# Second batch's rows loaded ahead of the third and fourth expert's weights, and its attention's place in the program worked out anew

## The chip, the cores and the metric

The kernel runs on one core of one Trainium2 chip. The metric is the device time of one execution in microseconds (us). Before the change it is 432.24 us, the median of three runs (428.54, 432.24 and 433.78). The profile shown here is that of one execution whose span, from the first to the last instruction, is 431.1 us.

## The reference

Attention over a sliding window of 128 positions plus four "sink" positions at the start, for 4 batches of 8 heads, 768 positions and 64 elements each. Its output, 3072 rows of 512, goes through four experts, each of two matrix products with a ReLU between; the experts' outputs are weighted and summed.

```python
# attention: q, k, v of shape (4, 8, 768, 64)
scores = (1 / sqrt(64)) * q @ k.transpose(0, 1, 3, 2)
keep   = (pos_k < 4) | ((pos_q - pos_k >= 0) & (pos_q - pos_k < 128))
a      = softmax(where(keep, scores, -1e9))
x      = (a @ v).transpose(0, 2, 1, 3).reshape(3072, 512)

# four experts: w1 (4, 512, 1024), w2 (4, 1024, 512)
p   = domain_probs / domain_probs.sum(-1, keepdims=True)
out = 0
for e in range(4):
    out += p[:, e:e+1] * (maximum(x @ w1[e], 0) @ w2[e])
```

## The kernel before

Everything is computed in bf16 with sums in fp32. The first batch comes in three pieces, is transposed on TensorE, and its attention starts early. The other batches are loaded by rows and transposed by the DMA engines. Batches are numbered from 0, so the second batch is batch 1; experts likewise.

```python
def load_rows(b):                          # batches 1 to 3
    for i, (name, src) in enumerate((("q", q), ("k", k))):
        x = sb.tile([P, NQB, H, D], BF16, name=f"{name}n", tag=f"{name}n", bufs=1)   # one buffer per name
        for tb in range(NQB):              # six loads of 128 KB (as bf16) each
            nc.gpsimd.dma_start(out=x[:, tb], in_=src[b, :, tb*P:(tb+1)*P, :].rearrange("h p d -> p h d"))   # L126
            lands(("rows", b), H * P * D * 4)
        ...
        nc.sync.dma_start_transpose(       # L132: qkT is what scores and sinks read
            out=qkT[b][:, i].rearrange("c t h p -> c (t h) p"),
            in_=x.rearrange("p t h d -> p (t h d)"))
    for hp in range(NHP):
        turned_at[b, 0, hp] = max(landed["rows", b], t["pe"]) + 11000.0

def load_v(b, ts):   ...  nc.gpsimd.dma_start(out=vx[b % 2][:, tb, :, 0:D], ...)     # L195, 128 KB each
def load_w1(e):      ...  nc.gpsimd.dma_start(out=w1_sb[e], ...)                     # L205, 1 MB as bf16
def load_w2(e):      ...  nc.gpsimd.dma_start(out=w2_sb[e], ...)                     # L210, 1 MB as bf16

def regroup(b, piece): ...  # batch 0: reads the same buffers "qn" and "kn" (DVE and ACT copies, L153)
def sink_keys(b):    ...    # POOL, L330: ksd from qkT, the first reader of a batch's transposed keys
def sinks(b, piece): ...    # PE, L349: sink scores from ksd and qkT
def scores(b, hp, g): ...   # PE, L370: window scores from qkT
def values(b, hp, g): ...   # PE, L414 and L421
def turn(b, hp, g):  ...    # PE, L446: gives xT, the experts' input
```

The order of instructions on TensorE is fixed when the program is built. A small model of times (`t`, `landed`, `turned_at`, `bank_free`, in ns) runs along; at each step the loop below emits the piece of work that the model holds to be ready: attention of the next batch ("att"), a first product with its ReLU ("first", L565) or a second product ("second", L600). The chip then runs this order as it stands and waits where the model was too hopeful. The numbers in `turned_at` thus move no data; they say from when on the model lets the batch's attention in.

```python
load_qk(0, 2)
load_v(0, (4, 5))
for e in (1, 2):
    load_w1(e)
    load_w2(e)

mix = Mixture()
att = Attention(0, ...)
while mix.more() or att.more():
    if not att.more() and ahead + 1 < B and (ahead == 0 or mix.done >= cols * ahead):
        ahead += 1
        load_rows(ahead)
        load_v(ahead, range(NQB))
        if ahead == 1:
            load_w1(3)
            load_w2(3)
        att = Attention(ahead, [("sinks", ahead, 0, 0)], range(NG))
        ...
    # ... the piece that the model holds to be ready is emitted
```

Of the kernel before, what the change touches and what calls it, by code (L numbers as in the profile page):

```python
# [16 lines left out]
def kernel(  # L17
# [27 lines left out]
    NQB = S // P  # L45
# [22 lines left out]
    t = {"pe": 0.0, "act": 0.0, "dve": 0.0}  # L68
# [22 lines left out]
    landed = {}  # L91
    dma = {"at": 2500.0}

    def lands(key, nbytes):
        dma["at"] += nbytes / 350.0
        landed[key] = dma["at"] + 1500
# [12 lines left out]
    nat, qkT, turned_at = {}, {}, {}  # L109
# [11 lines left out]
    def load_rows(b):  # L121

        for i, (name, src) in enumerate((("q", q), ("k", k))):
            x = sb.tile([P, NQB, H, D], BF16, name=f"{name}n", tag=f"{name}n", bufs=1)
            for tb in range(NQB):
                nc.gpsimd.dma_start(  # L126
                    out=x[:, tb], in_=src[b, :, tb * P:(tb + 1) * P, :].rearrange("h p d -> p h d"),
                )
                lands(("rows", b), H * P * D * 4)
            if b not in qkT:  # L130
                qkT[b] = sb.tile([P, 2, NQB, NHP, P], BF16, name="qkT", tag="qkT", bufs=2)
            nc.sync.dma_start_transpose(  # L132
                out=qkT[b][:, i].rearrange("c t h p -> c (t h) p"),
                in_=x.rearrange("p t h d -> p (t h d)"),
            )
        for hp in range(NHP):
            turned_at[b, 0, hp] = max(landed["rows", b], t["pe"]) + 11000.0

    def load_first():

# [52 lines left out]
    def load_v(b, ts):  # L193
        for tb in ts:
            nc.gpsimd.dma_start(  # L195
                out=vx[b % 2][:, tb, :, 0:D],
                in_=v[b, :, tb * P:(tb + 1) * P, :].rearrange("h p d -> p h d"),
            )
            lands(("v", b, tb), H * P * D * 4)
# [3 lines left out]
    def load_w1(e):  # L203
        w1_sb[e] = wpool.tile([P, NDB, F], BF16, name=f"w1_{e}", tag=f"w1_{e}")
        nc.gpsimd.dma_start(out=w1_sb[e], in_=moe_w1[e].rearrange("(db p) f -> p db f", p=P))  # L205
        lands(("w1", e), Dm * F * 4)

    def load_w2(e):
        w2_sb[e] = wpool.tile([P, NFB, Dout], BF16, name=f"w2_{e}", tag=f"w2_{e}")
        nc.gpsimd.dma_start(out=w2_sb[e], in_=moe_w2[e].rearrange("(fb p) d -> p fb d", p=P))  # L210
        lands(("w2", e), Dm * F * 4)
# [433 lines left out]
    sink_values(0)  # L645
    load_qk(0, 2)
    load_v(0, (4, 5))
    for e in (1, 2):
        load_w1(e)
        load_w2(e)  # L650

# [6 lines left out]
    ahead, upto, lead = 0, 0.0, 0.0  # L658
    while mix.more() or att.more():
        now = t["pe"]  # L660

        if not att.more() and ahead + 1 < B and (ahead == 0 or mix.done >= cols * ahead):
            ahead += 1
            load_rows(ahead)
            load_v(ahead, range(NQB))
            if ahead == 1:
                load_w1(3)
                load_w2(3)
            att = Attention(
                ahead, [("sinks", ahead, 0, 0)], range(NG),  # L670
            )
            upto = mix.done
        share = (cols * ahead - upto) * 0.96
        due = ahead == 0 or att.steps * share <= (mix.done - upto) * att.total
        opts = []
        if att.more():
            opts = [(max(r, now), 0 if due else 3, "att", step) for r, step in att.options()]
        f, s2 = mix.first_ready(), mix.second_ready()
        opts.append((max(f, now), 2, "first", None))
        opts.append((max(s2, now), 1 if mix.since >= 2 else 2.5, "second", None))  # L680
        r, _, kind, step = min(opts, key=lambda o: (o[0] > now + 40, o[0] if o[0] > now + 40 else 0, o[1]))
        if kind == "att":
            att.emit(step)
        elif kind == "first":
            mix.emit_first()
        else:
            mix.emit_second()
# [35 lines left out]
```

The softmax here doesn't subtract the row's maximum and nothing guards it: scores larger than these inputs give would overflow.

## Time and profile before

| | |
|---|---|
| time, median of three runs | 432.24 us |
| span of the profiled execution | 431.1 us |
| PE busy | 398.3 us (92%) |
| DVE, ACT, POOL busy | 168.1, 169.4, 76.0 us |
| work in the chain that ended last: PE, DMA, POOL | 77%, 17%, 4% |
| longest wait of PE | 15.7 us, once, in L349 |
| first products (L565), second products (L600) | 197.0 us in 1152, 183.0 us in 768 |
| DMA issues of weights, median time to landing | 8 of 1024 KB, 19.4 us |

How to read it: PE is TensorE, PEld its weight loads, DVE VectorE, ACT ScalarE, POOL GpSimd, SP SyncE; SPq is SP's queue, on which the DMA transposes and the output's writes are issued. A PE that is busy for 92% of the span leaves little besides its own work, so what can be won lies in its few idle stretches and in the stretches where its clock is granted at less than full speed. "DMA to landing" is the time from the issue of a transfer until its last part has arrived. Bytes of a transfer are counted as bf16.

### The profile page before, as it was taken

The numbers are of one execution on the slowest core, as the hardware profiler recorded it, in microseconds if no ns is written. First come the engines' busy times: TensorE is split into PE (matmuls) and PEld (weight loads), VectorE is DVE, ScalarE is ACT, GpSimd is POOL, SyncE is SP. The second block draws the span as 40 slices with busy tenths as digits, with TensorE's granted clock in tenths as the row PEclk, the third lists the DMA queues.
The fourth block names the chain that finished last, engine by engine and source line by source line (L and its number), as shares of the span: only waits on it lengthen the run. The fifth ranks groups of instructions, "written<-read, shape, count | busy, mean of one in ns | idle before, by whom it ended". The sixth has DMA issues, their size and how long they took to land.

```text
span 431.1 us, 6810 instructions
## 1 busy us (share of the span) xinstructions
PE 398.3 (92%) x2774; PEld 223.2 (52%) x2774; DVE 168.1 (39%) x348; ACT 169.4 (39%) x331; POOL 76.0 (18%) x124
## 2 busy tenths in 40 slices
PE   7599799049999999999999999999999999999996
PEld 3365466016766654555555554555555555555552
DVE  4667655006655523543434324433434222222222
ACT  3455300007643134454445335534445333333331
POOL 8834470059100007800000001000000000000000
PEclk9599889759999999999999999999999999999999
DMA  9999999999800159910000180000001110000012
GB/s 174 191 195 209 179 139 118 122 120 148 53 0 2 75 156 126 151 9 2 0 2 14 60 205 17 2 1 2 0 2 41 66 44 0 0 2 0 2 49 97
DMA packets 97251, 29.88 MB, mean 69 GB/s; under 512 B 85932, under 2 KB 92076, under 8 KB 97220
## 3 DMA queue, kind: packets, MB, share of 16 engines
q0 software_dynamic: 72832, 17.31, 43.7%
q1 hardware_dynamic: 24388, 12.14, 13.3%
q8 instruction: 21, 0.34, 0.3%
q14 instruction: 10, 0.08, 0.1%
HBM read 35.73 MB, written 6.29 MB: 97 GB/s over the span
## 4 chain that ended last, share of the span: by engine, by line
PE 77%; DMA 17%; POOL 4%; DVE 0%; issue 0%; ACT 0%; ACTq 0%; DVEq 0%; POOLq 0%
PE mop L600 36%; PE hps L565 35%; DMA w<-in_moe_w_dram 9%; DMA qkT<-kn 7%; PE sps L370 3%; PE od L421 2%; POOL vx L195 2%; DMA vx<-in_v_dram 1%; POOL kn L126 1%; PE tx L446 1%; PE od L414 1%; PE sps L349 0%; DVE ht L576 0%; POOL kn L115 0%; POOL qn L115 0%
## 5 line engine op out<-in xcount | busy, mean ns | idle before, releaser
L565 PE MATMUL hps<-xT,w 128*128 128x384 bf16 (+1 forms) x1152 | 197.0, 313 | 0.7 <-DVE ht L576 0.2
L574 ACT ACTIVATE ht<-hps 128x384 bf16<-128x384 f32 (+1 forms) x234 | 109.2, 471 | 188.5 <-PE hps L565 187.2
L600 PE MATMUL mop<-w,ht 128*128 128x512 bf16 x768 | 183.0, 382 | 0.0
L565 PEld LDWEIGHTS <-w 128*128 128x128 bf16 x1152 | 109.4, 99 | 66.5 <-issue 9.4
L600 PEld LDWEIGHTS <-ht 128*128 128x128 bf16 x768 | 73.6, 98 | 79.6 <-issue 4.3
L610 DVE SCALAR_TENSOR_TENSOR out_sb<-mop,scale_t,out_sb 128x512 f32<-128x512 f32 x72 | 54.1, 751 | 140.5 <-PE mop L600 140.1
L381 ACT ACTIVATE aT<-sps 128x1024 bf16<-128x1024 f32 (+1 forms) x46 | 44.0, 957 | 15.9 <-PE sps L370 15.6
L382 DVE TENSOR_TENSOR aT<-aT,mask 128x1024 bf16<-128x1024 bf16 (+1 forms) x46 | 30.0, 652 | 39.8 <-ACT aT L381 39.5
L608 DVE TENSOR_SCALAR out_sb<-mop,scale_t 128x512 f32<-128x512 f32 x24 | 18.0, 750 | 41.4 <-PE mop L600 41.1
L330 POOL TENSOR_TENSOR ksd<-qkT,half 128x8 bf16<-128x8 bf16 x16 | 2.7, 196 | 162.5 <-DMA qkT<-kn 162.5
L576 DVE TENSOR_SCALAR ht<-hps 128x256 bf16<-128x256 f32 (+1 forms) x54 | 23.1, 429 | 11.1 <-PE hps L565 9.3
L421 PE MATMUL od<-vx,aT 128*128 128x65 bf16 x352 | 21.2, 198 | 1.1 <-DVE aT L382 1.1
L195 POOL DMA_DIRECT2D vx<-in_v_dram x24 | 21.5, 960 | 0.0
L431 DVE TENSOR_TENSOR onat<-od,R 128x256 bf16<-128x256 f32 x48 | 20.4, 425 | 1.7
L421 PEld LDWEIGHTS <-aT 128*128 128x128 bf16 x352 | 18.0, 101 | 5.0 <-DVE aT L382 2.0
L446 PE MATMUL tx<-ident,onat 128*128 128x128 bf16 x96 | 13.6, 229 | 6.4 <-DVE onat L431 6.2
L370 PE MATMUL sps<-qkT 64*128 64x128 bf16 (+1 forms) x256 | 18.5, 248 | 1.0 <-ACT aT L381 0.7
L126 POOL DMA_DIRECT2D qn<-in_q_dram x18 | 15.9, 904 | 10.0 <-DVE R L428 8.1
L126 POOL DMA_DIRECT2D kn<-in_k_dram x18 | 15.9, 926 | 8.5 <-ACT aT L381 4.3
L349 PE MATMUL sps<-qkT,ksd 128*32 128x512 bf16 (+1 forms) x20 | 2.5, 390 | 15.7 <-POOL ksd L330 15.7
L153 ACT COPY xT<-tx 128x256 bf16<-128x256 bf16 x25 | 9.1, 373 | 16.6 <-PE tx L446 16.0
L446 PEld LDWEIGHTS <-onat 128*128 128x128 bf16 x96 | 8.3, 99 | 13.3 <-DVE onat L431 7.9
(60 smaller groups left out, 110.8 us busy)
## 6 DMA issues: line engine op xcount, KB each, us to landing
w<-in_moe_w_dram POOLq DMA_DIRECT2D x8, 1024.0 KB, 19.4
out_dram<-out_sb SPq DMA_DIRECT2D x24, 256.0 KB
vx<-in_v_dram POOLq DMA_DIRECT2D x24, 128.0 KB, 5.5
qn<-in_q_dram POOLq DMA_DIRECT2D x18, 128.0 KB, 4.2
kn<-in_k_dram POOLq DMA_DIRECT2D x18, 128.0 KB, 4.6
qraw<-in_q_dram SPq DMA_DIRECT2D x2, 256.0 KB
kraw<-in_k_dram SPq DMA_DIRECT2D x2, 256.0 KB
qn<-in_q_dram POOLq DMA_DIRECT2D x2, 256.0 KB, 9.6
```

Source lines behind the costliest of these rows:

```text
L126: nc.gpsimd.dma_start(out=x[:, tb], in_=src[b, :, tb * P:(tb + 1) * P, :].rearrange("h p d -> p h d"),)
L195: nc.gpsimd.dma_start(out=vx[b % 2][:, tb, :, 0:D], in_=v[b, :, tb * P:(tb + 1) * P, :].rearrange("h p d -> p h d"),)
L370: nc.tensor.matmul(sps[ph][:, c:c + nq * P], lhsT=T[pr, 1, kb, hp, :], rhs=T[pr, 0, qb:qb + nq, hp, :], start=True, stop=True,)
L381: nc.scalar.activation(out=a, in_=both[:, :, 0:w], func=AF.Exp, scale=scale)
L382: nc.vector.tensor_mul(a, a, m[:, None, :].to_broadcast([P, 2, w]))
L421: nc.tensor.matmul(od[:, qi, ph], lhsT=a[:, ph, c:c + P], rhs=vx[b % 2][:, kb, 2 * hp + ph, 0:DX], start=(g == 0 and i == 0), stop=(i == l ...
L446: nc.tensor.transpose(tx[:, qi], o[:, qi], ident)
L565: nc.tensor.matmul(hp_, lhsT=w1_sb[e][:, db, fb * P:(fb + 1) * P], rhs=xT[b, db][:, t0:t0 + n], start=(db == 0), stop=(db == NDB - 1),)
L574: nc.scalar.activation(out=ht, in_=hp_, func=AF.Relu)
L576: nc.vector.tensor_scalar(out=ht, in0=hp_, scalar1=0.0, scalar2=None, op0=ALU.max)
L600: nc.tensor.matmul(op, lhsT=hts[fb][:, off:off + P], rhs=w2_sb[e][:, fb, :], start=(fb == 0), stop=(fb == NFB - 1),)
L610: nc.vector.scalar_tensor_tensor(out=dst, in0=op, scalar=sc, in1=dst, op0=ALU.mult, op1=ALU.add,)
```

## The change

Before, the loads stand on POOL's queue in this order: weights of experts 1 and 2, rows of batch 1, values of batch 1, weights of expert 3. After, the rows and values of batch 1 go ahead of expert 2's weights, so that the transposes and the attention that wait for them can start sooner; the weights of experts 2 and 3 follow. Since the model's landing time of the rows moves forward too, and the weights now follow behind the transposes, the time that the model allows for the transposes of batch 1 is raised from 11,000 to 18,000 ns.

```diff
         for hp in range(NHP):
-            turned_at[b, 0, hp] = max(landed["rows", b], t["pe"]) + 11000.0
+            turned_at[b, 0, hp] = max(landed["rows", b], t["pe"]) + (18000.0 if b == 1 else 11000.0)
@@
     load_qk(0, 2)
     load_v(0, (4, 5))
-    for e in (1, 2):
+    load_w1(1)
+    load_w2(1)
+    load_rows(1)
+    load_v(1, range(NQB))
+    for e in (2, 3):
         load_w1(e)
         load_w2(e)
@@
             ahead += 1
-            load_rows(ahead)
-            load_v(ahead, range(NQB))
-            if ahead == 1:
-                load_w1(3)
-                load_w2(3)
+            if ahead > 1:
+                load_rows(ahead)
+                load_v(ahead, range(NQB))
             att = Attention(
                 ahead, [("sinks", ahead, 0, 0)], range(NG),
             )
```

## The prediction

> **What bounds the kernel now.** I read the page's busy times first: PE is busy for 398.3 of 431.1 us, so only its idle stretches and its slow clock can give anything back. The page's slices show where they are.
>
> ```profile
> PE   7599799049999999999999999999999999999996
> PEclk9599889759999999999999999999999999999999
> ```
>
> Each digit is one fortieth of the span, 10.8 us. From the tenth slice on PE is full. The eighth and ninth digits (0 and 4) are a hole at about 76 to 92 us, and the clock is below full in it and after it. PE's timeline in that stretch gives the hole its cause:
>
> ```profile
> 70.15 3.26 PE L565 MATMUL hps<-xT,w 128*128 128x256 bf16 x24
> 73.25 1.89 PE L600 MATMUL mop<-w,ht 128*128 128x512 bf16 x8
> 74.98 1.04 PE L565 MATMUL hps<-xT,w 128*128 128x256 bf16 x8
> 91.70 1.08 PE L349 MATMUL sps<-qkT,ksd 128*32 128x512 bf16 x4 [15.69 <-POOL ksd L330]
> ```
>
> The bracket says that PE sat idle for 15.69 us until POOL's ksd, which is the first reader of batch 1's transposed keys. The chain of work that ended last, in order of time, tells what POOL waited for:
>
> ```profile
> 24.68 25.02 DMA w<-in_moe_w_dram
> ...
> 58.03 4.54 DMA vx<-in_v_dram
> 62.57 28.74 DMA qkT<-kn
> ```
>
> The first line is w2 of expert 2, issued at 24.68 and landed at 49.70: the rows of batch 1 stand behind it. The last is the DMA transpose of the keys, issued at 62.57 and landed at 91.31. SP's timeline shows both transposes of batch 1 and, for comparison, those of batch 2:
>
> ```profile
> 54.92 7.41 SPq L132 DMA_TRANSPOSE qkT<-qn  x1
> 62.57 15.10 SPq L132 DMA_TRANSPOSE qkT<-kn  x1
> ...
> 155.86 3.04 SPq L132 DMA_TRANSPOSE qkT<-qn  x1
> 159.13 3.06 SPq L132 DMA_TRANSPOSE qkT<-kn  x1
> ```
>
> For batch 2, with no load beside it, POOL's ksd starts at 163.82, so both transposes together took about 163.8 - 155.9 = 7.9 us. For batch 1 they took 91.3 - 54.9 = 36.4 us: the loads of values and of expert 3's weights run beside them. That is the number on which my prediction turns.
>
> The clock costs as well. The table of stages at 2 us a row has the granted clock at 0.50 from 82 to 96 us and at 1.00 from 98. PE works from 91.70, so some 6.1 us of its work ran at half clock, which is a loss of about 3.05 us.
>
> **What the Trainium skill says.** "DMA: Bandwidth & Descriptors", section Queues, rings and completion order: each DMA engine takes turns between the queues that have work, one packet at a time. The trace agrees in kind: the transposes on SP's queue and the loads on POOL's queue both progress between 60 and 82 us, and neither waits for the other to finish (the fifth load of values landed at 73.3, the sixth at 81.8, between the starts and ends of the transposes). "TensorE: Matmul & The Clock Gate", section What's actually happening: the clock is halved after an idle window and comes back after a few us of sustained work, with windows of about 3.4 us. Here it fell some 5 us after the idle began (0.84 in the microsecond from 80) and came back about 6 us after work resumed.
>
> **The change part by part.**
>
> *Work.* No instruction is added or dropped. On PE the two programs have the same matmuls; the order differs only from a place shortly before batch 1's L349 until well into expert 3 of batch 0, after which it is the same.
>
> *When the rows land.* On POOL the rows wait for the buffer qn, which the DVE copy of batch 0's last piece frees (it starts at 32.95 and takes 0.42). Nothing moves that copy, so the first row load is issued near 33.67 as before. What changes is what stands ahead of it in the queue. From the issue times and the times to landing, w1 and w2 of expert 1 landed at 33.9 and 39.65 (22.35 + 17.3), w1 and w2 of expert 2 at 44.6 and 49.70. The last of the six q loads (issued at 39.95, 14.8 us to landing) landed at 54.75, which is 5.05 us behind expert 2's w2. After the change the q rows stand behind expert 1's w2 instead, so they should land 49.70 - 39.65 = **10.05 us earlier**, the last at about 44.7. POOL issues one row load in about 0.9 us and the queue takes them at about 0.87 us each, so issue isn't the limit.
>
> *How long the transposes take.* This is my choice. The same loads as before surround them: first the k rows, then six loads of values, then a w1 and a w2 of 1 MB each (now expert 2's in place of expert 3's), all issued with the same lead over the transposes. In the run before the second of these weights landed at 60.5 + 33.7 = 94.2, after the transposes' end at 91.31, so the load queue was never empty while they ran; the two further megabytes that now follow can't be felt before that point. I therefore keep the whole 36.4 us, not the 18 that the model assumes: end of the key transpose at 91.3 - 10.05 = 81.3, and L349 at 91.70 - 10.05 = **81.65**.
>
> *Where PE is by then.* In the new order L349 stands after the first 8 of the 24 first products that began at 70.15; their pace is 3.10/24 x 8 = 1.03 us, so PE arrives at 71.2. Before it arrived at 76.0. The 4.8 us between (16 first products 2.07, 8 second products 1.73, 8 first products 1.03) now stand behind L349. The wait becomes 81.65 - 71.2 = 10.5 us in place of 15.69, that is 5.2 us less. The diff's larger allowance doesn't let attention in later in PE's order: the model's landing moves forward by 12 us (4.2 MB of fp32 at its 350 bytes per ns) and the allowance grows by 7, so it is let in earlier.
>
> *The weights.* Expert 2's w1 should land at 88.4 - 10 = 78.4 and its w2 at 94.2 - 10 = 84.2, expert 3's about 5 and 10 us later (1 MB took 4.9 and 5.1 us without transposes beside it). In the new order PE has 12.2 us of work at full clock between L349 and the first use of expert 2's w1, at the trace's pace (1.73 us for eight products of 512 columns), and 21.8 us to its w2: not before 94 and 103. So no wait for weights.
>
> *The clock.* A wait of 10.5 us is still longer than the 5 us after which the clock fell, so I leave the loss of 3.05 us in.
>
> Sum: 432.24 - 5.2 = **427.0 us**, 1.2% less.
>
> **The rivals.**
>
> *The transposes get shorter.* If they take the 18 us that the change allows (44.7 + 18 = 62.7), they are over before PE arrives at 71.2, the whole 15.7 us goes and with it the clock's 3.05: 432.2 - 18.7 = 413.5. Anything under 27 us would suffice. For it: alone they take 7.9 us, and the new constant may have been measured. Against it: the same loads surround them.
>
> *The transposes starve until the load queue is empty.* Then the two further megabytes ahead of that moment hold them at about 91 as before, PE waits from 71.2 to 91.7, 20.5 us, and the time is 432.2 + 4.8 = 437. For it: the last 13.6 us of the key transpose (77.67, when SP had issued it, to 91.31) coincide with the two weights, and it ended close to the second's landing. Against it: it ended 2.9 us before that landing, and the two queues took turns earlier.
>
> *The weights become the wait.* If expert 2's w1 came at over 94, PE would wait a second time. Its lead of 16 us makes this unlikely, but a slower share for the loads would eat it up: each us past 94 costs one.
>
> *Attention stretches.* Between L349 and the merge of the two orders the short matmuls stand among fewer first products. Before, PE was idle for 0 of 20 us between 100 and 120, so I give this at most 1 us.
>
> **Range and chances.** The sum holds if the shift is a shift; the time in contention decides. The three runs before spread over 5.2 us, and contention beside a transpose is a likely source. 4 us either way gives 423 to 431; the rival of short transposes draws the lower end further down and the starving one sets the upper. Range 417 to 436. Faster by 2% means under 423.6, for which the key transpose must end 3.4 us sooner than reckoned, or the clock must hold: 0.28. Slower by 2% means over 440.9, which needs starving and a wait for weights together: 0.05.
>
> **What would show it right or wrong.** The page after should still have a hole in the seventh and eighth slice; PE's timeline an L349 at about 81.7 with about 10.5 us of idle time ahead of it, released by ksd. SP's timeline should have the q transpose at about 44.8 and the k transpose near 52.5, landing near 81.3 (the chain shows it). The stages should show half clock for some 6 us after L349. No wait for w should stand on PE. I'd be wrong if the q transpose doesn't start near 44.8 (the rows are then held by something else), if the k transpose takes far from 28.7 us, or if a second wait appears.

## The result, and the profile after

The changed kernel took 413.79, 413.86, 425.26 and 428.57 us in four executions, a median of 419.56 us; the kernel before had a median of 432.11 us beside it. The ratio is 0.9587, with an interval from 0.9485 to 0.969: faster. (The ratios here compare executions near the fastest of each kernel; for the changed kernel these are the two at 413.8, and the other two are part of what has to be explained.) The prediction was 427.0 us.

The profiled execution took 413.86 us, with a span of 412.2 us. In the page's slices (each digit a fortieth of the span, in tenths) PE has no hole any more, only the small dip of the start at 46 to 52 us:

```profile
PE   5599799999999999999999999999999999999996
PEclk9579989999999999999999999999999999999999
```

PE's timeline (start, duration, line, operation) has no bracket at L349, that is, no idle time ahead of it:

```profile
70.39 1.04 PE L565 MATMUL hps<-xT,w 128*128 128x256 bf16 x8
71.36 0.40 PE L349 MATMUL sps<-qkT,ksd 128*32 128x512 bf16 x4
```

SP's timeline has the two transposes of batch 1, and POOL's has ksd, which starts as soon as the keys are transposed (its bracket names the transpose that released it):

```profile
45.02 5.74 SPq L132 DMA_TRANSPOSE qkT<-qn  x1
51.00 9.53 SPq L132 DMA_TRANSPOSE qkT<-kn  x1
```

```profile
68.16 0.67 POOL L330 TENSOR_TENSOR ksd<-qkT,half 128x8 bf16<-128x8 bf16 x4 [9.19 <-DMA qkT<-kn]
```

The q transpose started at 45.02, 9.9 us sooner than before, and PE reached L349 at 71.36. Both are as predicted. But from the start of the q transpose to ksd it took 68.16 - 45.02 = 23.1 us, where before it took 91.45 - 54.92 = 36.5. The transposes were over three microseconds before PE asked for them. The span lost 431.1 - 412.2 = 18.9 us: the wait of 15.69 and the 3.05 of half clock after it make 18.74.

So two questions were open: why the same transposes, beside loads of the same kind, took 13 us less, and why other executions of the same program took 11 to 21 us more.

### The profile page after: what moved, and what is told of

The parts are those of the page before. It is cut to its first block, busy times and chain, and to the rows that moved or that the text cites. A ratio compares the mean times of both kernels' runs of the same rounds, so it can differ in the third digit from the quotient of the medians.

```text
span 412.2 us, 6809 instructions
## 1 busy us (share of the span) xinstructions
PE 393.9 (96%) x2774; PEld 221.2 (54%) x2774; DVE 166.9 (41%) x346; ACT 169.7 (41%) x333; POOL 75.7 (18%) x124
## 4 chain that ended last, share of the span: by engine, by line
PE 90%; DMA 3%; ACT 2%; DVE 2%; POOL 1%; issue 0%; ACTq 0%
PE hps L565 41%; PE mop L600 40%; PE sps L370 3%; DMA kn<-in_k_dram 3%; PE od L421 2%; PE tx L446 1%; ACT aT L381 1%; PE od L414 1%; PE tr L317 1%; POOL vx L195 0%; DVE onat L431 0%; PE sps L349 0%; DVE aT L382 0%; DVE qkT L153 0%; ACT ht L574 0%
## 5 line engine op out<-in xcount | busy, mean ns | idle before, releaser
L370 PEld LDWEIGHTS <-qkT 64*128 64x128 bf16 x256 | 7.7, 94 | 11.4 <-issue 9.1
```

Source lines behind the costliest of these rows:

```text
L370: nc.tensor.matmul(sps[ph][:, c:c + nq * P], lhsT=T[pr, 1, kb, hp, :], rhs=T[pr, 0, qb:qb + nq, hp, :], start=True, stop=True,)
```

## The experiments

In what follows, the **transpose time** is the time from the start of batch 1's q transpose on SP's queue to the start of POOL's ksd.

**The changed kernel again.** No edit.

> The changed kernel once more, as it is. Theory S (the time of batch 1's DMA transposes is set by the order of the loads: 23 us from the start of the q transpose in the changed order, 36 us in the order before): all times near 413.9 us; the profile has the k transpose landing near 68 and L349 near 71.4 without a wait. Theory J (the time beside the loads varies from one execution to the next, in either order): times spread from 413 to 429, each us of landing past 71 adding one, and 3 more for the clock where the wait is over 5 us.

Measured: 413.94, 425.44, 425.71, 427.52, 427.53 and 434.45 us, beside 431.45 for the kernel before. The profile is of the execution of 434.45. SP's timeline and PE's:

```profile
44.74 5.35 SPq L132 DMA_TRANSPOSE qkT<-qn  x1
53.72 20.91 SPq L132 DMA_TRANSPOSE qkT<-kn  x1
```

```profile
90.02 1.08 PE L349 MATMUL sps<-qkT,ksd 128*32 128x512 bf16 x4 [18.23 <-POOL ksd L330]
```

The q transpose started at the same time as in the other profile, but SP held the k transpose for 2.7 us longer, because the last k rows landed at 53.7 in place of 50.1, and ksd followed only at 89.77: a transpose time of 45.0 us. The order of the loads alone doesn't set this time: theory S fell. Of ten executions of the changed kernel in the two measurements, three took 413.8 to 413.9 and seven took 425 to 434. Their median is 425.6 us, about 6 us less than the kernel before: the ratio of 0.9587 above is that of the shorter case.

**The order of the loads without the allowance.** The changed kernel with

```diff
-            turned_at[b, 0, hp] = max(landed["rows", b], t["pe"]) + (18000.0 if b == 1 else 11000.0)
+            turned_at[b, 0, hp] = max(landed["rows", b], t["pe"]) + 11000.0
```

> The loads' order of the changed kernel with the allowance of 11000 as before. PE then reaches batch 1's L349 6.9 us of its work sooner than in the changed kernel, at about 64.5. Theory S: the k transpose lands at 68.1, L349 starts at about 68.5 after a wait of 4 us, the clock holds: 418. Theory J: the wait is between 4 and 17 us, 418 to 435, in steps with the landing.

Measured: 0.994 of the kernel before (0.991 to 0.998), 426 to 434 us. One further execution took 1401.85 us, and the profile happens to be of this one: its matmuls are about three times as long from beginning to end (PE busy 1369.8 us in place of 393.9), so its times say nothing of the order. I don't know what slowed it. The order alone brings next to nothing. By the reckoning of the expectation PE comes to L349 sooner, as the transposes do, and so waits all the same; no profile of an execution at the usual pace shows it.

**The allowance without the order.** The kernel before with the changed line of `turned_at`, nothing else.

> The loads' order of before with the allowance of 18000. PE reaches batch 1's L349 6.4 us of its work later than before, at about 82.4. Theory S: the k transpose lands at 91.3 as before, the wait is 9.3 in place of 15.7 us, time 432.2 - 6.4 = 425.8. Theory J: 413 to 427, with runs near 415 where the transposes happen to be as short as in the changed kernel's profile.

Measured: 420.42, 422.84, 424.49 and 425.32 us; 0.981 (0.977 to 0.985).

```profile
91.55 1.08 PE L349 MATMUL sps<-qkT,ksd 128*32 128x512 bf16 x4 [7.96 <-POOL ksd L330]
```

ksd started at 91.30, 36.7 us after the q transpose, as in the kernel before (36.5). PE only had more work ahead of L349. This is the part that the allowance brings by itself: half of the wait.

**A longer allowance.** The changed kernel with 30000 in place of 18000.

> The changed kernel with an allowance of 30000 for batch 1: PE reaches batch 1's L349 at about 82.1, in the same instruction order as in the run with the order of before and 18000. Theory S: the transposes were over at 68 anyway, so 413.9, the same as the changed kernel. Theory J: landings up to 82 are now covered, so 413.9 in nearly all runs, with a spread of about 1 us where the changed kernel spreads over 15.

Measured: 413.77, 413.87, 414.28, 414.31, 414.93 and 418.68 us; 0.962 (0.958 to 0.965). The profiled execution reached L349 at 83.97 without a wait; its transpose time was 23.6 us. The wider window covers what the transposes' time varies, so theory J holds as a description: what the changed kernel loses in its long executions is a wait at L349. Why the time varies it doesn't say. From here two theories stood against each other. Theory W: weights beside the transposes make them long. Theory V: the value loads do, with their many small packets.

**Weights held back.** The changed kernel, with the four weight loads moved behind `sink_keys`:

```diff
                     if b > 0:
                         sink_keys(b)
+                        if b == 1:
+                            for e in (2, 3):
+                                load_w1(e)
+                                load_w2(e)
@@
-    for e in (2, 3):
-        load_w1(e)
-        load_w2(e)
```

> The changed kernel, but the weights of experts 2 and 3 are issued on POOL behind batch 1's ksd, so they can't stand beside its transposes; the order on PE is unchanged. Theory W (the transposes are short while only value loads run beside them, and what isn't done when the weights begin goes slowly): the k transpose lands at 66 to 70 in every execution, L349 starts at 71.4 without a wait, expert 2's w1 lands near 75 where it is needed at 83.5: 414 in nearly all executions. Theory V (the value loads, with their many small packets, make the long case; the weights are innocent): a spread of 413 to 434 as in the changed kernel.

Measured: 412.93 to 414.63 us in six executions; 0.959 (0.956 to 0.963). The spread of 20 us is gone.

```profile
45.12 6.78 SPq L132 DMA_TRANSPOSE qkT<-qn  x1
52.13 10.30 SPq L132 DMA_TRANSPOSE qkT<-kn  x1
```

```profile
67.33 0.67 POOL L330 TENSOR_TENSOR ksd<-qkT,half 128x8 bf16<-128x8 bf16 x4 [16.88 <-DMA qkT<-kn]
```

The transpose time is 22.2 us with the values beside it. Theory V fell as the cause of the long case; the values do cost some 10 us of transpose time (a run below without them has 12.0).

**Weights held back in the kernel before.** The order of the loads and the allowance are those of before; only expert 3's weights move behind `sink_keys`:

```diff
                         sink_keys(b)
+                        if b == 1:
+                            load_w1(3)
+                            load_w2(3)
@@
             load_v(ahead, range(NQB))
-            if ahead == 1:
-                load_w1(3)
-                load_w2(3)
```

> The kernel before, but expert 3's weights are issued on POOL behind batch 1's ksd; order of the other loads and order on PE as before. Theory W: q transpose at 54.8, k transpose landed 23 to 25 us later, at 78 to 80, wait of L349 2 to 4 us in place of 15.7 and the clock holds: 415 to 419. Theory V: landing at 91.3 as before, 432. Theory S (order of the loads alone): 432.

Measured: 416.02 to 416.52 us in four executions; 0.965 (0.960 to 0.970).

```profile
55.37 7.41 SPq L132 DMA_TRANSPOSE qkT<-qn  x1
63.02 9.51 SPq L132 DMA_TRANSPOSE qkT<-kn  x1
```

```profile
77.54 0.86 PE L349 MATMUL sps<-qkT,ksd 128*32 128x512 bf16 x4 [1.41 <-POOL ksd L330]
```

The transposes start when they did before, but take 77.29 - 55.37 = 21.9 us in place of 36.5, and the wait falls from 15.69 to 1.41. Three lines moved, with neither part of the change, bring all but 2 us of what the changed kernel reaches at its best (413.8).

**Values held back, weights beside the transposes.** The changed kernel, with batch 1's value loads issued behind `sink_keys` (the model's book-keeping is left as it was, so that PE's order is the same).

```diff
-    load_v(1, range(NQB))
+    load_v(1, range(NQB), issue=False)     # only books the landing
@@
                         sink_keys(b)
+                        if b == 1:
+                            load_v(1, range(NQB), book=False)   # issues
```

> The changed kernel, but batch 1's values are issued on POOL behind batch 1's ksd, so that the k rows and then only weights stand beside the transposes. The profile is what counts, not the time, since PE will have to wait for the values. Theory W: the k transpose takes long although no small packets are beside it, landing at 75 or later (over 30 us from the start of the q transpose at 45). Theory V: it lands at 60 or sooner, under 15 us.

```profile
45.09 15.16 SPq L132 DMA_TRANSPOSE qkT<-qn  x1
60.48 30.50 SPq L132 DMA_TRANSPOSE qkT<-kn  x1
```

```profile
97.99 0.67 POOL L332 TENSOR_TENSOR ksd<-qkT,half 128x8 bf16<-128x8 bf16 x4 [49.10 <-DMA qkT<-kn]
```

The transpose time is 52.9 us, the longest of all and as theory W forecast, and the one execution took 443.44 us. Expert 2's and 3's weights landed at 75.4, 85.2, 90.4 and 97.2: the transposes were over only when the last weight was.

**Both held back.** The changed kernel, with values and weights behind `sink_keys`, values first.

```diff
                         sink_keys(b)
+                        if b == 1:
+                            load_v(1, range(NQB))
+                            for e in (2, 3):
+                                load_w1(e)
+                                load_w2(e)
@@
-    load_v(1, range(NQB))
-    for e in (2, 3):
-        load_w1(e)
-        load_w2(e)
```

> The changed kernel, but values and weights both are issued behind batch 1's ksd: the transposes have only the k rows beside them. Both theories: k rows landed at 50, q and k transpose over 8 to 10 us after, landing at about 55 to 58; L349 at 71.4 without a wait; values landed by 64 and expert 2's w1 by 70, long before their use: 414 in every execution.

Measured: 413.41 to 414.52 us; 0.959 (0.955 to 0.963). ksd started at 56.96, so the transpose time is 12.0 us, 5 of which the k rows were still landing in. PE doesn't ask before 71, so nothing more is won by it than by holding the weights alone.

**Half of the weights, whole and in small pieces.** Two runs beside each other tell what it is in a weight load that costs so much. The first is the kernel before with w1 of expert 3 where it was and w2 held back:

```diff
                         sink_keys(b)
+                        if b == 1:
+                            load_w2(3)
@@
                 load_w1(3)
-                load_w2(3)
```

> The kernel before, with only w1 of expert 3 ahead of the transposes' end and w2 held behind batch 1's ksd. Theory W: half of the weights' traffic beside the tail, so the k transpose lands between that of the run with both held (77.2) and that of before (91.3), at 83 to 90: wait of L349 7 to 14 us, 423 to 431.

The second has the same, and w1 of expert 3 is written in runs of 256 bytes, four transfers with a gap behind each run, in place of runs of 2 KB:

```diff
+            w1_sb[e] = wpool.tile([P, NDB, NFB, 136], BF16, ...)          # e == 3
+            for db in range(NDB):
+                nc.gpsimd.dma_start(
+                    out=w1_sb[e][:, db, :, 0:P],
+                    in_=moe_w1[e, db * P:(db + 1) * P, :].rearrange("p (c f) -> p c f", f=P))
```

> As the run beside it with w1 of expert 3 ahead, but this w1 is written in runs of 128 elements (256 bytes) with a gap behind each, in four transfers, so that the same bytes go in more and shorter packets. Theory W as turns by packet: each turn of the weights costs the transposes less, so they land at 78 to 82 and the time is 416 to 422. If weights slow the transposes by their bytes, whatever the packets: the same as the run beside it within 2 us.

The first took a median of 429.0 us, 0.994 (0.992 to 0.996), the second 419.5 us, 0.972 (0.968 to 0.976). POOL's ksd of the first and of the second:

```profile
87.66 0.67 POOL L330 TENSOR_TENSOR ksd<-qkT,half 128x8 bf16<-128x8 bf16 x4 [27.10 <-DMA qkT<-kn]
```

```profile
79.33 0.67 POOL L337 TENSOR_TENSOR ksd<-qkT,half 128x8 bf16<-128x8 bf16 x4 [9.90 <-DMA qkT<-kn]
```

The packets by size, on the page of each (in all, and how many of them are under 512 bytes, under 2 KB, under 8 KB):

```profile
DMA packets 97252, 29.88 MB, mean 70 GB/s; under 512 B 85933, under 2 KB 92077, under 8 KB 97221
```

```profile
DMA packets 100883, 29.88 MB, mean 71 GB/s; under 512 B 90076, under 2 KB 96220, under 8 KB 100852
```

Between 2 and 8 KB there are 97221 - 92077 = 5144 packets in the first and 4632 in the second, 512 fewer, and under 512 bytes there are 4143 more: w1 went in some 4096 small packets in place of 512 large ones. The transpose times are 32.8 and 24.3 us: 8.4 us less for the same bytes. It is the length of the weights' packets that slows the transposes, and not their bytes alone. The last part of the small w1 landed at 83.3, 4 us after ksd, so weights stood in the queue all the while.

The turns can be counted in the traces. Each pair of lines has, for SP's queue (q1, here the transposes) and POOL's (q0, the loads), the packets, the MB and the time that the packets took as a share of that of the 16 DMA engines (packets overlap, so the shares can add up to over 100%): first the changed kernel's shorter case from 58 to 62 us, with values beside the transposes, then its longer case from 64 to 88 us, with weights beside them.

```profile
q1 hardware_dynamic: 1664, 0.43, 80.0%
q0 software_dynamic: 1664, 0.21, 79.5%
```

```profile
q0 software_dynamic: 2391, 3.26, 92.1%
q1 hardware_dynamic: 2368, 0.60, 34.0%
```

In both, the transposes move one packet (256 bytes) for each packet of the loads. Beside values (128 bytes to a packet) that gives them 0.43 MB in 4 us; beside weights (1 or 2 KB) 0.60 MB in 24 us, a quarter of that pace. It isn't one for one everywhere: in the run with the values held, from 50 to 60 us, the transposes moved 1231 packets beside 304 of the loads, and both went slowly. That stretch stays unexplained.

**Weights held back, allowance of 11000.** The run with held weights, with the `turned_at` line of before.

> The changed order with the weights of experts 2 and 3 held behind ksd, and the allowance back at 11000: PE reaches batch 1's L349 at about 64.5 to 65. Theory W: the k transpose lands at 67 in every execution, so a wait of 2 to 3 us and no fall of the clock: 416 to 417, where the order with 11000 and weights beside the transposes gave 426 to 434.

Measured: 417.15 to 418.88 us; 0.970 (0.966 to 0.974).

```profile
66.91 0.86 PE L349 MATMUL sps<-qkT,ksd 128*32 128x512 bf16 x4 [3.29 <-POOL ksd L330]
```

The profiled execution, of 417.15 us, has a wait of 3.29 us and is 3.3 us above the 413.89 of the run with 18000. The three others are some 1.6 us higher still. Their mean granted clock is 0.969 to 0.970 in place of 0.977, so the clock may have fallen after the wait; no profile shows it. With the weights held back the allowance is worth 3 to 5 us, and 18000 is enough.

The runs in one table, sorted by what stood beside the transposes of batch 1. Transpose time and wait are those of the profiled execution, the time is the run's median or, for the two cases of the changed kernel and the run with the values held, that of the one execution:

| beside the transposes | run | q transpose to ksd, us | wait at L349, us | time, us |
|---|---|---|---|---|
| nothing (batch 2, kernel before) | | 8.0 | | |
| k rows | both held | 12.0 | 0 | 413.6 |
| k rows, values | weights held, 11000 | 21.7 | 3.3 | 418.8 |
| k rows, values | before, weights held | 21.9 | 1.4 | 416.1 |
| k rows, values | weights held | 22.2 | 0 | 413.9 |
| k rows, values, w1 in small runs | before | 24.3 | 3.1 | 419.5 |
| k rows, values, w1 | before | 32.8 | 11.5 | 429.0 |
| k rows, values, w1, w2 | kernel before | 36.5 | 15.7 | 432.1 |
| k rows, values, w1, w2 | before, allowance 18000 | 36.7 | 8.0 | 423.7 |
| k rows, values, four weights | changed kernel, allowance 30000 | 23.6 | 0 | 414.3 |
| k rows, values, four weights | changed kernel, the shorter case | 23.1 | 0 | 413.86 |
| k rows, values, four weights | changed kernel, the longer case profiled | 45.0 | 18.2 | 434.45 |
| k rows, four weights | values held | 52.9 | 26.6 | 443.4 |

## Why the prediction was wrong

The direction was right, and the time lies in the range, but the gain was 12.6 us by the medians of the first measurement in place of 5.2: 18 us in the changed kernel's shorter case, and about 6 us over all ten executions.

- **When the rows land: right.** Predicted 10.05 us sooner and the q transpose at about 44.8; it started between 44.74 and 45.60 in seven profiles with the changed order.
- **Where PE is by then: right.** Predicted 71.2, found 71.36.
- **How long the transposes take: the step that failed.** I kept "the whole 36.4 us", with the reason that "the same loads as before surround them". The loads were the same in kind, and yet this time is no constant of them. It is 22 us while values run beside the transposes, and what isn't done when the weights begin is drawn out by them, to 36.5 in the kernel before and to 45.0 in one execution of the changed kernel, but to 23.1 in another. The mis-sized term is 36.4 us, with 23.1 measured in the profiled execution. My rival of short transposes (413.5) gave the time of that execution, but it rested on 18 us, a constant that "may have been measured"; what made the transposes short is that they were nearly through when the weights began (see below).
- **The two further megabytes: wrong too.** I held that they couldn't be felt. In the profiled long case the key transpose ended at about 89.8, as the third of the four weights landed (89.7), so they can be. My rival of starving transposes, with an end at about 91 and a time of 437, comes near this execution (434.45), though here they ended 4.8 us before the fourth weight.
- **The clock: wrong only through the wait.** With no wait there was no fall of the clock at L349.
- **The weights: right.** Even where they were issued only at 68 us, no wait for them appeared.

Seven of ten executions of the changed kernel lie at 425 to 434, about the 427.0 that the long transposes gave, but that is in part luck: in the one profiled the transposes took 45.0 us and PE waited 18.2, where I had 36.4 and 10.5. I treated as constant what varies from one execution to the next.

What the runs show, then: the change wins by the length of its transposes, which start sooner and, by luck in some executions, escape the weights; and its allowance hides part of the rest. "DMA: Bandwidth & Descriptors", section Queues, rings and completion order, has the DMA engines take turns by packet. The runs agree: in the two stretches counted above the turns are one packet for one, so the queue with the long packets takes more of the time, and shortening the packets of w1 gave back 8.4 of the 10.8 us by which w1 lengthened the transposes. The page has an engine drain a packet of typically nine to seventeen descriptors before it changes queues; the counts here are of the profile's packets, of 128 bytes to 2 KB, and whether these are the same thing isn't shown.

**Short and long in the traces.** The six value loads of a batch are 6144 packets and its two transposes are 6144 too, so, turn for turn, they would end together unless one side gets a lead. The transpose time goes with how many of the transposes' packets are left when the first packet of a weight moves: some 350 in the shorter case (transpose time 23.1 us), 2000 in the kernel before (36.5), 3000 in the longer case (45.0) and 5900 with the values held (52.9). In the longer case the lead can be seen: the k transpose started 2.7 us later, behind the late k rows, and from 54.4 to 58.1 us the loads moved 4254 packets and SP's queue 32. In the shorter case the same pause, from 55.1 to 56.2, let only 1282 packets of the loads by.

**What stays open.** Why the last k rows landed 3.6 us later in that execution, and whether the same happened in the other long ones, of which there is no profile. Nor is it shown why the kernel before had 2000 packets left with a pause of only 1.1 us, and why none of its executions had the short case.

## What to carry to other kernels

A transfer's duration beside other traffic can't be carried from one order of loads to another: ask what will stand in the other queue at the moment when it ends, and how long that traffic's packets are. Bulk loads that aren't needed soon belong behind the transfer that PE waits for, here by issuing them after its first reader: this made 416 of 432 us by three lines moved, and made the changed kernel's best time its usual one (413.9). A time that differs by 15 us between executions of one program is a result to look into, for a margin in the schedule (here 30000) can cover it.

## What the runs showed of the hardware that I had not expected

- A pair of DMA transposes of 0.79 MB each takes 8.0 us alone, 22 us beside loads in small packets and 52.9 us beside weight loads, which is 6.6 times as long.
- PE's clock stayed at 1.00 through waits of 1.4 and 3.3 us in two profiles (weights held in the kernel before, and with the allowance of 11000), but after one of 3.1 us (w1 in small runs) it was at 0.56 and 0.59 in the four microseconds from 80. In these profiles the length of the wait alone doesn't tell whether the clock falls.
- One execution of the 75 of the changed kernel and the experiments ran its matmuls at about a third of their pace from beginning to end, at a granted clock that the profile gives as full.
